# Early V loads into idle K buffers, and gathers in float32, in an attention and squared-ReLU kernel on one core

## The chip, the cores and the metric

The kernel runs on one core of a Trainium2 chip. The metric is device microseconds of one execution, median of three runs. TensorE is PE here, VectorE DVE, ScalarE ACT, GpSimd POOL; SyncE (SP) only issues DMAs.

## The reference

Batch 8, 8 heads, 576 positions, head size 64, 8 global positions. Attention within a window of 32 positions to either side, with 8 global rows and columns, then a dense layer to 2048, a squared ReLU and a dense layer back to 512:

```
scores = q @ k.T / sqrt(64)
mask   = (abs(i - j) <= 32) | is_global[i] | is_global[j]
attn   = softmax(where(mask, scores, -1e9)) @ v        # (8, 8, 576, 64) float32
x      = attn.transpose(0, 2, 1, 3).reshape(4608, 512)
out    = (s * relu(x @ w_in)**2 + b) @ w_out           # w_in 512x2048, w_out 2048x512
```

## The kernel before

The attention goes by pairs of heads: 32 pairs, counted from 0, four to a batch. A pair has five column chunks of 120 keys, with the 8 global keys in front of each (120 + 8 = 128 rows). Of a pair, `qk` (L530) makes the scores of a chunk on PE, ACT takes the exponent (`em` of pairs 0 to 4 at L544, `e` of later ones at L547; DVE multiplies those with a mask at L548), and `pvq` (L550) multiplies with V. `norm_steps` (L577) divides by the sums and puts the result into `xt`, the input of the dense layers. These run on PE as small pieces ("quanta", `moe_quanta` L644): L659 for x @ w_in into `psh`, ACT's L681 and DVE's L684 for the squared ReLU, L693 for the second product. A number of quanta stands behind each chunk of attention, so that PE has work while ACT and DVE are busy. All engines run in the order in which the code is written; every instruction waits for those it depends on by semaphores, and an engine that waits holds up all that stands behind it on that engine.

Inputs come in three ways.

- K and Q of pairs 0 to 7 are loaded as six rows to a partition into `six` (pair 0 on the hardware queues, 1 to 7 by `load_kq` L166 on POOL's queue, cast to bfloat16 on the way). K of pairs 8 and on is loaded in float32 into `natk` (four slots, `load_nat` L174, on SP's queue), cast by ACT into `natb` (`round_k` L199) and transposed by a DMA (`turn_k` L233). K of pair 8 is the first that goes this way; it is loaded at pair 4 and cast in chunk 1 of pair 6. So slots of `natk` are idle until then, but for pair 0's K at the start, which uses slot 0 and part of slot 1.
- V of every pair is loaded in float32 into `natv` (four slots, two DMAs of 150 KB to a pair) and cast into `vring` (five slots) by ACT or POOL: `cast_v` L242. V of pair 4 goes into slot 0, which is free when V of pair 0 has been cast. Rows 0 to 7 of `natv` are filled once (L267) with any numbers, since the cast reads all 128 rows; `put_v` (L435) then overwrites them in `vring` with the global rows.
- The rows of K, Q and V at the global positions are gathered by indirect DMAs on POOL's queue (`gather` L312) into `gf`, cast to bfloat16 on the way. `globals_of` (L397) gives the steps that turn them: PE transposes (L409), DVE copies (L413, L416).

POOL's queue also brings `w_in` (two halves, `load_w_in`) and `w_out` (four quarters, `load_w_out`). SP's and POOL's DMAs take turns on 8 semaphores each: a DMA waits until the one 8 before it on its queue has landed.

The first part of the program is `first_pair` (L848) for pairs 0 to 4. Within it ACT casts V of pair 0 (in chunk 1), POOL V of pairs 1 to 3 (L962 to L965), and ACT V of pair 4 in the last chunk of pair 4 (L879), followed by V of pair 5 (L793) and then by the first ReLUs. SP's queue holds V of pairs 0 to 6, then two fills with zeros (L998, L1001: rows 96 to 127 of the Q tiles and of `natb`; the first waits for PE's transposes of pair 5), V of pair 7, then K, Q and V of pairs 8, 9, 10 and so on. In chunk 1 of pair 6, ACT casts V of pair 6 and then K of pair 8.

Of the kernel before, what the change touches and what calls it, by code (L numbers as in the profile page):

```python
# [9 lines left out]
FP32 = mybir.dt.float32  # L10
# [6 lines left out]
P = 128  # L17
B, H, S, D = 8, 8, 576, 64
NG = 8
# [50 lines left out]
def kernel(  # L70
# [95 lines left out]
    def load_kq(p):  # L166
        bi, hp = divmod(p, 4)
        for t in "kq":
# [3 lines left out]
            )  # L172

    def load_nat(eng, t, p):  # L174
        bi, hp = divmod(p, 4)
        if t == "q":
            dst = natq[:].rearrange("p n h j d -> p n (h j d)")[:, :, 0 : NCH * 2 * D]
            dst = dst.rearrange("p n (c h d) -> p n c h d", c=NCH, h=2)
        else:
            dst = natv if t == "v" else natk  # L180
        r = NG if t == "v" else 0
        for hh in range(2):
            o = src[t][bi, 2 * hp + hh, 0, 0].offset

            runs = [(0, NCH, KC)]
            if p == NPAIR - 1 and hh == 1:
                runs = [(0, NCH - 1, KC), (NCH - 1, 1, S - KC * (NCH - 1))]
            for c, nch, n in runs:
                eng.dma_start(  # L189
                    out=dst[r : r + n, p % NV, c : c + nch, hh],  # L190
                    in_=bass.AP(
                        tensor=src[t].tensor, offset=o + c * KC * D,
                        ap=[[D, n], [KC * D, nch], [1, D]],
                    ),
                )
# [43 lines left out]
    def load_v(eng, p):  # L239
        load_nat(eng, "v", p)  # L240

    def cast_v(eng, p):  # L242
        eng(out=vring[:, p % NVR], in_=natv[:, p % NV])  # L243

# [28 lines left out]
    )  # L273
    load_v(nc.sync, 0)
    load_v(nc.sync, 1)
    load_v(nc.sync, 2)
    load_v(nc.sync, 3)

# [33 lines left out]
    def gather(bb, ts="kq"):  # L312

        if bb not in gfs:
            gfs[bb] = globp.tile([P, 3, D], BF16, tag="gf", name="gf")
        for t in ts:
            i = "kqv".index(t)
            nc.gpsimd.indirect_dma_start(
                out=gfs[bb][:, i], out_offset=None,
                in_=src[t].rearrange("b h s d -> (b h s) d"),  # L320
                in_offset=IndirectOffsetOnAxis(ap=grow[bb][:], axis=0),
            )
# [74 lines left out]
    def globals_of(bb):  # L397

        gb = gfs[bb]
        gkt[bb] = globp.tile([P, D], BF16, tag="gkt", name="gkt")  # L400
        if bb == 0:
            gvx[0] = const.tile([NG, 16 * D], BF16, name="gvx", tag="gvx")

        def turn():
# [27 lines left out]

        return turn, lambda: move(0), lambda: move(1)

# [492 lines left out]
    build_biases((0,))  # L927

    gather(0, "kqv")
    load_kq(3)  # L930
    load_kq(4)
# [18 lines left out]
    def clear6():  # L950
# [4 lines left out]
        0: [lambda: build_biases((1, 2)), clear6],  # L955
        1: [lambda: build_biases((3, 4)), lambda: cast_v(A, 0)],
        3: [clears],
        4: [lambda: select(1)],
    })
    flush()  # L960
    load_kq(5)
    cast_v(G, 1)  # L962
    cast_v(G, 2)
    load_w_in(1)
    cast_v(G, 3)  # L965
# [5 lines left out]
    load_w_out(1)  # L971
    load_v(nc.sync, 4)
    load_v(nc.sync, 5)
    load_v(nc.sync, 6)
    for p in (1, 2, 3, 4):
        first_pair(p, {
            2: [steps0[0]],
            4: [*steps0[1:], flush],
        } if p == 1 else {
# [14 lines left out]
    for i in (1, 2, 3):  # L994
# [8 lines left out]
        in_=view(dummy[96:P], [0, NV * NCH * P // DM], [1, DM]),  # L1003
    )
    load_v(nc.sync, 7)
    gather(1)
# [24 lines left out]
    for p in range(4, NPAIR):  # L1031
# [47 lines left out]
        if p % 8 > 4 and p + 3 < NPAIR:  # L1079
            if p % 8 == 6:  # L1080
                pass
            elif p % 8 == 7:
                at(3, globals_of((p + 3) // 8)[0])
        for s in {12: (2, 3, 4), 13: (7,), 14: (2, 4, 7)}.get(p, (2, 3, 4, 7)):
# [54 lines left out]
```

## Time and profile before

| what | number |
|---|---|
| time, median of 3 runs | 352.94 us (352.19 to 353.15) |
| the profiled execution: its own time, its span | 352.61 us, 350.9 us |
| busy share of the span: PE, DVE, ACT, POOL | 93%, 66%, 62%, 18% |
| shares of the chain that ended last | PE 81%, DVE 7%, DMA 5% |
| DMA: bytes, mean rate | 50.41 MB, 144 GB/s |
| share of 16 DMA engines, SP's queue and POOL's queue | 57.5%, 15.7% |

The shares are means over two very different stretches. Up to about 66 us the first pairs are set up, weights come in and PE has gaps; behind it PE is busy almost without a break. A DMA share over 1.00 in the windows means that packets of several queues were in flight on an engine at once. In the timelines "x2" are instructions merged into a row, and the brackets show how long the engine was idle before it and what ended that.

### The profile page before, as it was taken

Reading aid. Unit: us, or ns where it says so; the run is one execution under the profiler, and the core shown is the slowest. Engines: PE = TensorE matmul, PEld = TensorE weight load, DVE = VectorE, ACT = ScalarE, POOL = GpSimd, SP = SyncE. Lnnn points to the kernel's source line nnn. Section 1 sums busy time; section 2 is a strip of 40 time slices with the busy share of each in tenths; the row PEclk is TensorE's granted clock in tenths of the full one; section 3 lists DMA queues with packets and bytes.
Section 4 is the critical chain, followed back from the end, with each engine's and each line's share of the span. In section 5 each row is a group of like instructions: output and inputs, shape, how many; then the busy total and the mean of one; then the engine's idle time right before and its main releaser. Section 6 shows DMA issues by size and latency. Waiting matters only on the chain.

```text
span 350.9 us, 8468 instructions
## 1 busy us (share of the span) xinstructions
PE 327.3 (93%) x3130; PEld 172.7 (49%) x3175; DVE 231.8 (66%) x662; ACT 217.5 (62%) x453; POOL 64.4 (18%) x148
## 2 busy tenths in 40 slices
PE   5688698899999999999999999999999999999995
PEld 3244344355455444467645544554457544444444
DVE  6477766776868888877677767676767553413421
ACT  5458558746896579657875887588648604603600
POOL 7942641114001601130005000300020010000000
PEclk9999989999999999999999999999999999999999
DMA  8999999999997999999388877972530011011002
GB/s 168 210 204 198 189 199 202 200 174 223 178 186 157 216 198 192 210 168 175 50 184 203 206 159 152 262 178 67 157 111 2 2 62 61 1 61 60 0 34 89
DMA packets 125938, 50.41 MB, mean 144 GB/s; under 512 B 112544, under 2 KB 119360, under 8 KB 125888
## 3 DMA queue, kind: packets, MB, share of 16 engines
q1 hardware_dynamic: 116470, 38.78, 57.5%
q0 software_dynamic: 9072, 10.65, 15.7%
q8 instruction: 25, 0.41, 0.5%
q10 hardware_dynamic: 354, 0.43, 0.4%
q14 instruction: 17, 0.14, 0.1%
HBM read 42.27 MB, written 9.44 MB: 147 GB/s over the span
## 4 chain that ended last, share of the span: by engine, by line
PE 81%; DVE 7%; DMA 5%; issue 2%; ACT 2%; SPq 1%; another core or an unknown queue 1%; ACTq 0%; DVEq 0%
PE pso L693 32%; PE psh L659 32%; PE pss L535 6%; PE po L565 6%; DMA natk<-in_k_dram 4%; PE pst L461 1%; PE pst L474 1%; SPq L189 1%; DVE qbd L519 1%; DVE wsum L1016 1%; DVE kt L486 1%; DMA row<-in_moe_b_dram 1%; PE pss L534 1%; ACT em L544 1%
## 5 line engine op out<-in xcount | busy, mean ns | idle before, releaser
L659 PE MATMUL psh<-xt,win_t 128*128 128x512 bf16 (+4 forms) x685 | 136.7, 341 | 0.8 <-issue 0.2
L693 PE MATMUL pso<-wout_t,g 128*128 128x512 bf16 (+1 forms) x569 | 132.9, 373 | 2.1 <-issue 1.4
L681 ACT ACTIVATE r<-psh 128x512 bf16<-128x512 f32 x144 | 86.4, 602 | 59.2 <-PE psh L659 49.8
L659 PEld LDWEIGHTS <-win_t 128*128 128x128 bf16 x704 | 64.2, 98 | 57.8 <-issue 4.9
L684 DVE TENSOR_TENSOR g<-r 128x512 bf16<-128x512 bf16 x144 | 60.5, 431 | 39.6 <-ACT r L681 39.0
L693 PEld LDWEIGHTS <-g 128*128 128x128 bf16 x592 | 56.0, 98 | 59.1 <-issue 1.0
L547 ACT ACTIVATE e<-pss 128x384 bf16<-128x384 f32 (+2 forms) x135 | 62.8, 469 | 34.5 <-PE pss L535 31.7
L535 PE MATMUL pss<-qbd,kt 128*128 128x384 bf16 (+2 forms) x160 | 50.4, 318 | 9.9 <-DVE qbd L835 4.3
L548 DVE TENSOR_TENSOR em<-e,mask 128x384 bf16<-128x384 bf16 (+2 forms) x135 | 45.6, 339 | 14.7 <-ACT e L547 12.8
L636 POOL COPY xt<-xg 128x4 bf16 (+1 forms) x72 | 18.8, 262 | 174.9 <-DVE xt L611 169.2
L713 DVE SCALAR_TENSOR_TENSOR osb<-pso,spread,bias_row 128x512 f32<-128x512 f32 (+1 forms) x25 | 18.1, 726 | 29.7 <-PE pso L693 27.0
L535 PEld LDWEIGHTS <-kt 128*128 128x128 bf16 x160 | 15.7, 99 | 25.1 <-DVE qbd L835 4.0
L611 DVE TENSOR_TENSOR xt<-po,rep 128x480 bf16<-128x480 f32 (+2 forms) x60 | 24.3, 446 | 0.3 <-ACT rep L621 0.3
L514 DVE COPY qbd<-pst 64x600 bf16<-64x600 bf16 x38 | 17.8, 468 | 9.2 <-PE pst L461 8.6
L519 DVE COPY qbd<-pst 64x600 bf16<-64x600 bf16 x20 | 15.6, 780 | 5.8 <-PE pst L474 2.9
L200 ACT CAST natb<-natk 120x640 bf16<-120x640 f32 x24 | 17.7, 738 | 1.4 <-DMA natk<-in_k_dram 1.4
L544 ACT ACTIVATE em<-pss 128x384 bf16<-128x384 f32 (+2 forms) x25 | 11.1, 462 | 9.9 <-PE pss L540 5.2
L243 ACT CAST vring<-natv 128x640 bf16<-128x640 f32 x20 | 14.8, 742 | 3.8 <-DMA natv<-in_v_dram 3.8
L565 PE MATMUL po<-em,vring 128*32 128x160 bf16 (+3 forms) x840 | 16.9, 218 | 0.0
L618 ACT ACTIVATE ln<-po 128x324 f32<-128x324 f32 (+1 forms) x30 | 13.1, 435 | 3.8 <-PE po L565 3.8
L621 ACT ACTIVATE rep<-ln 128x324 f32<-128x324 f32 (+1 forms) x32 | 15.2, 475 | 0.1
L224 ACT CAST sixq<-natq 120x640 bf16<-120x640 f32 x19 | 14.3, 753 | 0.0
(124 smaller groups left out, 228.1 us busy)
## 6 DMA issues: line engine op xcount, KB each, us to landing
natv<-in_v_dram SPq DMA_DIRECT2D x63, 150.0 KB
natk<-in_k_dram SPq DMA_DIRECT2D x47, 150.0 KB
out_dram<-osb SPq DMA_DIRECT2D x23, 256.0 KB
natq<-in_q_dram SPq DMA_DIRECT2D x37, 150.0 KB
wst<-in_moe_w_out_dram POOLq DMA_DIRECT2D x8, 512.0 KB, 3.8
out_dram<-osbh SPq DMA_DIRECT2D x9, 256.0 KB
win_t<-in_moe_w_in_dram POOLq DMA_DIRECT2D x4, 512.0 KB, 12.4
wout_t<-in_moe_w_out_dram POOLq DMA_DIRECT2D x4, 512.0 KB, 10.5
```

The costliest lines, as they stand in the source:

```text
L519: eng(out=view(qbufs[p % 3][r, hh], [P, NCH], [HB + NG, 2], [NJ, n], [1, NJ]), in_=view(ps[r], [2 * n, NCH], [n, 2], [1, n], [NP6, NJ]),)
L535: nc.tensor.matmul(ps[:], ktile[p][:, P * c : P * c + P], qbufs[p % 3][:, :, LO[c] : HI[c]], start=p == 0 or p >= NCH, stop=p > 0,)
L547: nc.scalar.activation(e[:], ps[:], AF.Exp, scale=SCALE)
L548: later.append(lambda: nc.vector.tensor_mul(em[:], e[:], masks[c]))
L565: nc.tensor.matmul(po[DH * j : DH * j + DH, a : a + n], view(vring[:, p % NVR, c, hh, part - 1 :], [2, DH]) if part else onesb[:], emt[(p, ...
L611: nc.vector.tensor_tensor(out=view(xt[:, 2 * g, x0 + t0 :], [NXT, 2], [w, runs], [1, w]), in0=view(po[:, STEP[blk] + col :], [STEP[blk], 2 ...
L636: nc.gpsimd.tensor_copy(out=xt[:, h, S * (bi % NX) : S * (bi % NX) + S][:, :, ds(greg_p[i], 1)], in_=xgs[bi][:, h, i : i + 1],)
L659: nc.tensor.matmul(psh[:, d0 : d0 + n], win_t[:, a, f * P : f * P + P], xt[:, a, x0 : x0 + n], start=(a == 0 and j == 0), stop=(a == 3), s ...
L681: nc.scalar.activation(r[:], psh, AF.Relu)
L684: later.append(lambda g=g, r=r: nc.vector.tensor_mul(g[:], r[:], r[:]))
L693: nc.tensor.matmul(pso[:, 0:nn], gl[f][:, u * P : u * P + P], wout_t[:, f, n0 : n0 + nn], start=(f == 0), stop=(f == 15),)
L713: nc.vector.scalar_tensor_tensor(out=osb[:, 0:nn], in0=pso[:, 0:nn], scalar=s_bc, in1=bias_row[:, n0 : n0 + nn], op0=OP.mult, op1=OP.add,)
```

## The change

V of pairs 4 and 5 (the fifth and sixth) is loaded into slots 2 and 3 of `natk`, straight behind V of pair 3, so that it waits for no cast; a further small DMA fills rows 0 to 7 of these slots. V of pair 6 goes to `natv` behind the zero fills. The gathers keep float32, and a new DVE cast `round_g` makes the bfloat16 tile `gb`; the three gathers of batch 0 and 1 stand behind K and Q of pair 3 on POOL's queue. V of pair 0 is cast by POOL, not by ACT. The zero fills `clears` stand at chunk 2 of pair 0 in place of chunk 3, and the steps of `globals_of` are spread over chunks 1, 2 and 4 of pair 1.

```diff
+    def v_slot(p):
+        return p - 2 if p in (4, 5) else p % NV
...
             dst = natv if t == "v" else natk
-        r = NG if t == "v" else 0
+            if t == "v" and p in (4, 5):
+                dst = natk
+        r, n = (NG if t == "v" else 0), v_slot(p) if t == "v" else p % NV
...
     def cast_v(eng, p):
-        eng(out=vring[:, p % NVR], in_=natv[:, p % NV])
+        eng(out=vring[:, p % NVR], in_=(natk if p in (4, 5) else natv)[:, v_slot(p)])
...
-    load_v(nc.sync, 0)
-    load_v(nc.sync, 1)
-    load_v(nc.sync, 2)
-    load_v(nc.sync, 3)
+    nc.sync.dma_start(
+        out=natk[0:NG, 2:4].rearrange("p n c h d -> p (n c h d)"),
+        in_=bass.AP(
+            tensor=v.tensor, offset=v.offset,
+            ap=[[2 * NCH * 2 * D, NG], [1, 2 * NCH * 2 * D]],
+        ),
+    )
+    for p in range(6):
+        load_v(nc.sync, p)
...
-            gfs[bb] = globp.tile([P, 3, D], BF16, tag="gf", name="gf")
+            gfs[bb] = globp.tile([P, 3, D], FP32, tag="gf", name="gf")
...
-        gb = gfs[bb]
+        gb = globp.tile([P, 3, D], BF16, tag="gb", name="gb")
...
+        n = 2 if bb else 3
+
+        def round_g():
+            nc.vector.tensor_copy(out=gb[:, 0:n], in_=gfs[bb][:, 0:n])
...
-        return turn, lambda: move(0), lambda: move(1)
+        return round_g, turn, lambda: move(0), lambda: move(1)
...
+    load_kq(3)
     gather(0, "kqv")
-    load_kq(3)
     load_kq(4)
...
-        1: [lambda: build_biases((3, 4)), lambda: cast_v(A, 0)],
-        3: [clears],
+        1: [lambda: build_biases((3, 4))],
+        2: [clears],
...
+    cast_v(G, 0)
     cast_v(G, 1)
+    load_w_in(1)
     cast_v(G, 2)
-    load_w_in(1)
     cast_v(G, 3)
...
-    load_v(nc.sync, 4)
-    load_v(nc.sync, 5)
-    load_v(nc.sync, 6)
     for p in (1, 2, 3, 4):
         first_pair(p, {
-            2: [steps0[0]],
-            4: [*steps0[1:], flush],
+            1: [steps0[0]],
+            2: [steps0[1]],
+            4: [*steps0[2:], flush],
...
+    load_v(nc.sync, 6)
     load_v(nc.sync, 7)
...
             if p % 8 == 6:
-                pass
+                steps = globals_of((p + 4) // 8)
+                at(7, steps[0])
             elif p % 8 == 7:
-                at(3, globals_of((p + 3) // 8)[0])
+                at(3, steps[1])
```

SP's queue from the fill of `natv` to K and Q of pair 8, before (`natv<-in_v_dram` are V loads, two to a pair; `dummy` is the source of the zero fills):

```order
L267 DMA natv<-in_v_dram 8x2560
L189 DMA natv<-in_v_dram 120x5x64 x14
L998 DMA sixq<-dummy 32x10x384
L1001 DMA natb<-dummy 32x5x512
L189 DMA natv<-in_v_dram 120x5x64 x2
L189 DMA natk<-in_k_dram 120x5x64 x2
L210 DMA natq<-in_q_dram 96x2x384
```

The same stretch with the change:

```order
L272 DMA natv<-in_v_dram 8x2560
L279 DMA natk<-in_v_dram 8x1280
L194 DMA natv<-in_v_dram 120x5x64 x8
L194 DMA natk<-in_v_dram 120x5x64 x4
L1012 DMA sixq<-dummy 32x10x384
L1015 DMA natb<-dummy 32x5x512
L194 DMA natv<-in_v_dram 120x5x64 x4
L194 DMA natk<-in_k_dram 120x5x64 x2
L215 DMA natq<-in_q_dram 96x2x384
```

One small fill is added in front; of the 14 V loads in a row 12 stand there now, the last four of them into `natk`, and the two of pair 6 stand behind the zero fills, ahead of pair 7's.

POOL behind its loads for pair 2, before (`sixk`, `sixq` are K and Q of a pair, here of pairs 3 and 4; `gf` are the gathers):

```order
L318 DMA gf<-in_k_dram,grow_163 128x64
L318 DMA gf<-in_q_dram,grow_163 128x64
L318 DMA gf<-in_v_dram,grow_163 128x64
L169 DMA sixk<-in_k_dram 96x2x384
L169 DMA sixq<-in_q_dram 96x2x384
L169 DMA sixk<-in_k_dram 96x2x384
L169 DMA sixq<-in_q_dram 96x2x384
```

With the change:

```order
L169 DMA sixk<-in_k_dram 96x2x384
L169 DMA sixq<-in_q_dram 96x2x384
L328 DMA gf<-in_k_dram,grow_168 128x64
L328 DMA gf<-in_q_dram,grow_168 128x64
L328 DMA gf<-in_v_dram,grow_168 128x64
L169 DMA sixk<-in_k_dram 96x2x384
L169 DMA sixq<-in_q_dram 96x2x384
```

The three gathers went behind K and Q of pair 3. Further down, two V casts still stand ahead of the second half of w_in (of pairs 0 and 1 now, 1 and 2 before), and two behind it in place of one.

DVE in pair 1, from the copy of pair 2's Q to the next K, before (`gkt`, `gqd` are filled from PE's transposes `psg` of the gathered rows):

```order
L830 CAST kt<-psg 128x5x8
L835 CAST qbd_119<-psg 64x5x8 x2
L519 COPY qbd_120<-pst 64x5x2x60 x2
L413 COPY gkt<-psg 128x64
L416 COPY gqd_121<-psg 64x64 x2
L486 COPY kt<-pst 128x5x120
```

With the change:

```order
L845 CAST kt<-psg 128x5x8
L850 CAST qbd_119<-psg 64x5x8 x2
L534 COPY qbd_120<-pst 64x5x2x60 x2
L417 CAST gb<-gf 128x192
L428 COPY gkt<-psg 128x64
L431 COPY gqd_121<-psg 64x64 x2
L501 COPY kt<-pst 128x5x120
```

The new cast stands between the Q copies and the copy of `gkt`; PE's transposes, which stood ready by then, come behind it now. The zero fills of `clears` keep their place among DVE's instructions.

## Rows read from the trace of the kernel before

**Rows 1.** page, part 2: DMA busy (tenths) and GB/s, 40 slices
```profile
DMA  8999999999997999999388877972530011011002
GB/s 168 210 204 198 189 199 202 200 174 223 178 186 157 216 198 192 210 168 175 50 184 203 206 159 152 262 178 67 157 111 2 2 62 61 1 61 60 0 34 89
```

**Rows 2.** windows: start:end, length, busy us of each engine (instructions), PEclk, DMA, GB/s
```profile
36.00:40.80 4.80, 4.64 (x42) 2.14 (x41) 3.62 (x15) 1.01 (x2) 3.55 (x11) 1.00 1.16 207
40.80:44.20 3.40, 0.74 (x4) 0.39 (x4) 2.07 (x7) 3.32 (x8) 2.79 (x4) 1.00 1.18 161
44.20:47.60 3.40, 3.18 (x20) 1.42 (x18) 1.33 (x5) 2.06 (x6) 1.80 (x4) 0.50 1.24 199
51.00:55.00 4.00, 3.33 (x54) 1.68 (x53) 3.57 (x13) 3.23 (x7) 1.51 (x4) 1.00 1.16 220
57.10:62.60 5.50, 4.70 (x41) 2.02 (x40) 5.03 (x14) 4.47 (x10) 0.81 (x2) 1.00 1.04 213
66.00:350.90 284.90, 278.29 (x2488) 147.39 (x2524) 187.47 (x521) 176.44 (x364) 30.77 (x75) 1.00 0.65 132
```

**Rows 3.** timeline of ACT: start us, us, what, [idle before <-releaser]
```profile
15.46 0.72 ACT L243 CAST vring<-natv 128x640 bf16<-128x640 f32 x1
...
36.37 0.72 ACT L243 CAST vring<-natv 128x640 bf16<-128x640 f32 x1
40.88 0.72 ACT L243 CAST vring<-natv 128x640 bf16<-128x640 f32 x1 [3.79 <-DMA natv<-in_v_dram]
...
55.93 0.72 ACT L200 CAST natb<-natk 120x640 bf16<-120x640 f32 x1 [1.44 <-DMA natk<-in_k_dram]
```

**Rows 4.** timeline of PE, 40 to 65 us
```profile
40.20 0.59 PE L659 MATMUL psh<-xt,win_t 128*128 128x512 bf16 x2
43.45 0.32 PE L535 MATMUL pss<-qbd,kt 128*128 128x384 bf16 x1 [2.66 <-ACT e L547]
...
57.10 0.28 PE L535 MATMUL pss<-qbd,kt 128*128 128x272 bf16 x1 [0.75 <-ACT e L547]
...
62.62 0.47 PE L535 MATMUL pss<-qbd,kt 128*128 128x320 bf16 x2 [0.82 <-DVE qbd L449]
...
64.69 0.32 PE L535 MATMUL pss<-qbd,kt 128*128 128x384 bf16 x1 [0.73 <-ACT e L547]
```

**Rows 5.** chain of waits up to 70 us: start us, us, what
```profile
7.50 3.83 another core or an unknown queue
...
42.04 13.51 DMA natk<-in_k_dram
```

**Rows 6.** timeline of SP's queue: V of pair 4, K of pair 8
```profile
16.21 0.33 SPq L189 DMA_DIRECT2D natv<-in_v_dram  x1
...
42.04 4.69 SPq L189 DMA_DIRECT2D natk<-in_k_dram  x2
```

**Rows 7.** waits of SP's queue up to 70 us: us in total, times, longest
```profile
SPq L189 <- ACT vring L243: 4.0, 1, 4.0
SPq L998 <- PE pst L474: 3.4, 1, 3.4
```

**Rows 8.** timeline of DVE, 4 to 22 us
```profile
4.51 0.83 DVE L896 CAST sixk<-natk 96x768 bf16<-96x768 f32 x1
...
11.32 0.20 DVE L830 CAST kt<-psg 128x40 bf16<-128x40 f32 x1 [3.82 <-remote]
...
19.74 1.57 DVE L519 COPY qbd<-pst 64x600 bf16<-64x600 bf16 x2 [1.09 <-PE pst L474]
21.24 0.17 DVE L413 COPY gkt<-psg 128x64 bf16<-128x64 bf16 x1
```

**Rows 9.** timeline of PE, pair 1: transposes of the gathered rows
```profile
20.06 0.25 PE L409 MATMUL psg<-ident,gf 64*64 64x64 bf16 x4
```

**Rows 10.** timeline of POOL: first gather; casts of V
```profile
7.03 1.05 POOL L318 DMA_INDIRECT gf<-in_k_dram,grow  x1 [0.30 <-DVE kt L486]
...
16.10 1.40 POOL L243 CAST vring<-natv 128x640 bf16<-128x640 f32 x2
```

More of the change, by code (lines that the diff above doesn't have):

```diff
@@ L187, in load_nat @@
                 runs = [(0, NCH - 1, KC), (NCH - 1, 1, S - KC * (NCH - 1))]
-            for c, nch, n in runs:
+            for c, nch, rows in runs:
                 eng.dma_start(
-                    out=dst[r : r + n, p % NV, c : c + nch, hh],
+                    out=dst[r : r + rows, n, c : c + nch, hh],
                     in_=bass.AP(
                         tensor=src[t].tensor, offset=o + c * KC * D,
-                        ap=[[D, n], [KC * D, nch], [1, D]],
+                        ap=[[D, rows], [KC * D, nch], [1, D]],
                     ),
```

## The prediction

> **What bounds the kernel now.** I first read the windows of the whole trace. From 66 us on PE is busy for 278.29 of 284.90 us [rows 2], so nothing but the stretch ahead of 66 us can move the end by much: there PE has gaps, and whatever moves the moment at which PE gets its last late input moves the end by as much. Two more things are to be seen in that stretch. The DMA engines are busy nearly without a break: 9 tenths in slices 2 to 11 of the page, with 189 to 210 GB/s in each up to 70 us [rows 1], and a share of 1.16 or more in every window from 36 to 55 us [rows 2]. And the TensorE clock, which is 1.00 elsewhere, is 0.50 (1.2 in place of 2.4 GHz) from 44.2 to 47.6 us, just after a stretch of 3.4 us in which PE was busy for 0.74 us [rows 2].
>
> Then I looked for the gaps. PE stands still for 2.66 us from 40.79 to 43.45 us, waiting for ACT [rows 4]. ACT in turn had stood for 3.79 us in front of the cast of pair 5's V, whose DMA had not landed; it starts at 40.88 us [rows 3]. That is the wait at which the change aims. The next ones are 0.75 us at 57.10, 0.82 at 62.62 and 0.73 at 64.69 us [rows 4]. The first of them is a DMA's again: ACT waits 1.44 us for pair 8's K and casts it at 55.93 us [rows 3]. The chain of waits does not go through V of pair 5 at all. It goes through pair 8's K: 13.51 us from its issue at 42.04 us to its landing at 55.55 us [rows 5, 6]. So of two waits of ACT for a DMA the chain holds the second. This is the main thing in my forecast: the first wait is longer, but it ends 15 us earlier, and time won there only counts if pair 8's K comes earlier too.
>
> **The change part by part.** *V of pairs 4 and 5 earlier.* SP's queue stood 4.0 us for the cast of pair 0's V before it could issue pair 4's at 16.21 us [rows 6, 7]. With the slots in `natk` that wait is gone. If all behind it moves up by the 4.0 us, pair 5's V lands at 40.88 - 4.0 = 36.9 us; ACT is ready for it at 36.37 + 0.72 = 37.09 us [rows 3]. The wait is then gone. If the loads keep half of their gain (w_in's loads share the engines), it shrinks to 3.79 - 2.0 = 1.8 us. PE would get back up to 2.66 us of idle time and what the half clock took: PE was busy for 3.18 us of that window [rows 2], which at 2.4 GHz is 1.6 us of work, so 1.6 us. Together up to 4.3 us, between 37 and 55 us of the program.
>
> *Pair 8's K.* In SP's order V of pair 6 moves from ahead of the zero fills to behind them, but still stands ahead of K of pair 8. The same bytes go ahead of this K as before, and the engines were never idle before it. Added are the fill of `natk` (8 rows of 1280 float32, 41 kB) and the wider gathers (128 rows x 64 x 2 bytes more, three times, 49 kB): 90 kB, at 199 GB/s [rows 2] 0.45 us. Against that, the window from 40.8 to 44.2 us moved 161 GB/s where its neighbours moved 207 and 199 [rows 2]: about 40 GB/s x 3.4 us = 136 kB, 0.7 us, which a steadier flow can fill. So pair 8's K lands 0.25 us earlier by this, between 0.45 us later and 0.7 us earlier by its two terms. ACT and PE arrive there up to 4.3 us earlier, and wait. PE's 0.75 us there becomes about 4 us.
>
> *The clock.* A wait of 2.66 us was followed by half the clock [rows 2, 4]; one of 4 us will be too, now behind 55 us. In the window from 57.1 to 62.6 us PE is busy for 4.70 of 5.50 us, and DVE for 5.03 [rows 2]: DVE sets the pace there, and PE has 0.82 + 0.73 = 1.55 us of waiting up to 65 us that can absorb the 1.6 us of the slow stretch. Between 0 and 1.6 us, I take 0.2, by the waits that are there to be filled.
>
> *The gathers and the new cast.* The new cast of 128x192 stands between two measured ones, 0.20 us for 128x40 and 0.83 for 96x768 [rows 8]; by their columns some 0.33. PE's transposes at 20.06 us [rows 9] must now come behind it. DVE ends its Q copies at 21.31 us; then cast 0.33 and transposes 0.25, so `gkt` comes some 0.6 us later than its 21.24 us [rows 8]. PE waits too. Below: 0, if the stage reaches DVE earlier. It delays the zero fills of SP, which wait for PE [rows 7], by up to 0.6 us, while the DMA engines still work off w_out; hence I count it at 0, and at 0.6 if that cover is gone. In pairs 6, 14 and 22 the same cast stands in stretches where PE is never short: nothing. The gathers go behind two loads for pair 3 and land some 2 us later; they are needed by 21 us. Nothing.
>
> *V of pair 0 on POOL.* ACT loses 0.72 us at 15.46 us [rows 3], where it waits for PE afterwards anyway; POOL's casts cost 0.70 us each [rows 10], and POOL's next loads queue up behind others. `clears` keeps its place in DVE's order. Both nothing.
>
> Sum against the profiled execution's own 352.61 us: -0.25 + 0.2 = -0.05, so 352.56, 0.4 under the median of 352.94, whose runs spread over 0.96 us. I forecast 352.6, no change that can be measured; 0.3% is 1.06 us and about what a measurement of this kernel can tell.
>
> The Trainium skill has a rule that speaks against the change. TensorE: Matmul & The Clock Gate, in HAM oscillation, says that a wait for a DMA in front of dense matmuls makes them start at half the clock, and that the cost returns with every such wait. The trace agrees at 44.2 us (0.50). By that rule a long wait at pair 8's K would be paid in full; this is the second rival.
>
> **The rivals.** *The early wait counts in full.* If pair 8's K lands 4 us or more earlier (because the queue ahead of it is served better, or because the unexplained wait at 7.50 us goes), PE keeps what it wins: 2.66 + 1.6 + 0.75 - 0.6 = 4.4 us, 348.2 us. That wait of 3.83 us, in which DVE stood before `kt` at 11.32 us, began when POOL issued the first gather, at 7.03 us [rows 5, 8, 10]. For this rival speaks that SP gets 4.0 us earlier to everything behind; against it the full DMA engines [rows 1]. 14%. In between, with K of pair 8 1 to 3 us earlier: some 350.8 us, 20%.
>
> *Slower: a late K and a slow clock.* PE arrives early at pair 8's K and waits more than the 2.66 us that were enough for the half clock; the K itself lands 0.45 us later for the added bytes and 0.6 us for the later zero fills; and PE's slow stretch is not covered by DVE: 1.6 us. Sum 2.7 us, 355.3 us. It decides as soon as K lands no earlier and more than 1 us of the slow stretch shows. For it speaks that the clock did fall at 44.2 us [rows 2]; against it that DVE is the busier engine behind 57 us. 26%.
>
> *The change doesn't do what it says:* V of pair 5 still lands at 38 us or later, the wait shrinks to 1.8 us, and pair 8's K decides as before: 352.6 us, no change. It is within the likeliest case's result; 8% of the 40% below.
>
> **How the numbers follow.** Forecast (K of pair 8 decides, no change) 40%, its own range 351.4 to 354.0; full gain 14%; partial gain 20%; slower 26%. Of the forecast's 40 some 2 end below 351.88 and 2 above 354.0. Of the partial gain 3 stay within 0.3%. Of the slower case 2 stay within it. So faster 14 + 17 + 2 = 33, slower 24 + 2 = 26, same 41. The range from 349.2 to 355.2 us leaves out most of the full gain and the upper part of the slower case, some 2 in 10.
>
> **What would show it.** In the profile after: no wait of ACT before the two V casts at 37 us, and a clock of 1.00 from 44 to 48 us (the first step). ACT's wait before the first cast of `natk` into `natb` grows from 1.44 to about 5 us, ending near 55.5 us, with PE idle before it and a clock of 0.50 behind it (the second and third). The DVE cast of `gb` takes 0.2 to 0.8 us, and PE's transposes behind it start some 1.5 us later than 20.06 (the fourth). I am wrong if that cast of pair 8's K starts more than 1 us before 54.9 us, or if the chain of waits no longer holds the K loads.

## The result and the profile after

The changed kernel takes 354.87 us (median of 20 runs, 352.64 to 357.61) against 352.88 us before (20 runs, 352.16 to 354.81); the ratio is 1.0056, 95% interval 1.0035 to 1.0078. It is slower by some 2 us; I had forecast no change. The profiled execution took 356.62 us (span 354.9 us against 350.9), so its 4.0 us are more than the usual loss; a second profile (e11) is shown beside it below. Ratios leave out executions far above a kernel's fastest and medians do not, so for e17 and e19 the two differ.

The page of the changed kernel, DMA busy and GB/s in 40 slices, to be laid beside [rows 1]:
```profile
DMA  9999999999999899999099867983440011011002
GB/s 157 219 202 199 165 194 188 184 190 178 204 192 166 186 200 221 209 176 174 21 177 235 194 145 164 247 192 78 151 129 2 2 61 60 0 60 60 0 32 89
```
Slices are 8.9 us long: the fifth, from 35.5 to 44.4 us, has 165 GB/s where it had 189. The windows of [rows 2], in the same columns, place it:
```profile
36.00:40.80 4.80, 4.16 (x40) 2.00 (x41) 4.51 (x18) 2.66 (x7) 2.61 (x10) 1.00 1.02 174
40.80:44.20 3.40, 2.42 (x13) 1.13 (x13) 2.88 (x9) 3.38 (x8) 3.10 (x3) 1.00 0.99 148
44.20:47.60 3.40, 3.19 (x72) 1.87 (x73) 2.06 (x6) 2.07 (x6) 3.10 (x4) 1.00 1.13 160
...
57.10:62.60 5.50, 2.80 (x19) 0.98 (x20) 2.39 (x5) 3.97 (x9) 0.72 (x1) 0.50 0.89 184
66.00:350.90 284.90, 280.17 (x2495) 148.16 (x2532) 190.27 (x529) 178.62 (x368) 31.64 (x76) 1.00 0.66 133
```
In the first three the engines move 174, 148 and 160 GB/s where they moved 207, 161 and 199: (207 - 174) x 4.8 + 13 x 3.4 + 39 x 3.4 = 335 kB less, 1.7 us at 199 GB/s. The shortfall lies there alone: up to 36 us the two kernels move 195 (before) and 194 GB/s, from 36 to 48 us 191 and 163, and from 48 us to the landing of pair 8's K 201 and 204. The clock is 1.00 at 44 to 48 us now, and 0.50 at 57 to 63.

ACT's casts that wait for a DMA, answering to [rows 3]: V of pairs 4 and 5, V of pair 6, K of pair 8:
```profile
37.30 0.72 ACT L248 CAST vring<-natk 128x640 bf16<-128x640 f32 x1
40.06 0.72 ACT L248 CAST vring<-natk 128x640 bf16<-128x640 f32 x1 [2.04 <-DMA natk<-in_v_dram]
52.63 0.72 ACT L248 CAST vring<-natv 128x640 bf16<-128x640 f32 x1 [1.20 <-DMA natv<-in_v_dram]
58.63 0.72 ACT L205 CAST natb<-natk 120x640 bf16<-120x640 f32 x1 [5.27 <-DMA natk<-in_k_dram]
```
The wait for V of pair 5 fell from 3.79 to 2.04 us; the one for pair 8's K rose from 1.44 to 5.27 and ends 2.70 us later. PE's timeline, for [rows 4, 9], with waits of 0.98, 5.89 and 0.73 us where there were 2.66, 0.75 and 0.73; ahead of them the transposes of the globals, which waited for nothing listed before:
```profile
20.38 0.25 PE L424 MATMUL psg<-ident,gb 64*64 64x64 bf16 x4 [1.75 <-DVE gb L417]
...
42.63 0.32 PE L550 MATMUL pss<-qbd,kt 128*128 128x384 bf16 x1 [0.98 <-ACT e L562]
...
59.80 0.39 PE L550 MATMUL pss<-qbd,kt 128*128 128x272 bf16 x1 [5.89 <-ACT e L562]
67.89 0.32 PE L550 MATMUL pss<-qbd,kt 128*128 128x384 bf16 x1 [0.73 <-ACT e L562]
```
PE is 0.82 us early at 42.63 us, 2.70 late at 59.80, 3.20 late at 67.89 (the half clock took 0.5). The SP queue's timeline, for [rows 6, 7], says why:
```profile
13.82 8.84 SPq L194 DMA_DIRECT2D natk<-in_v_dram  x4
38.25 0.76 SPq L1012 DMA_DIRECT2D sixq<-dummy  x1
39.06 0.60 SPq L1015 DMA_DIRECT2D natb<-dummy  x1
39.76 5.09 SPq L194 DMA_DIRECT2D natv<-in_v_dram  x4
44.89 6.76 SPq L194 DMA_DIRECT2D natk<-in_k_dram  x2
```
SP is through with the issue of its last early V load at 22.66 us and then stands for 15.6 us before the zero fills, until PE has done with the transposes of pair 5. Before, V of pair 6 stood ahead of them, so this wait was 3.4 us [rows 7]. Now V of pairs 6 and 7 comes behind them instead of pair 7's alone, and pair 8's K is issued at 44.89 instead of 42.04 us. The chain of waits goes through these transposes, the fills, SP's issues and the DMA of pair 8's K, and through a second DMA far behind:
```profile
37.84 0.66 PE pst L489 x24
...
39.06 0.60 SPq L1015
...
42.52 2.33 SPq L194
44.89 2.95 SPq L194
47.88 10.68 DMA natk<-in_k_dram
...
145.76 6.37 DMA wst<-in_moe_w_out_dram
```
The last is a piece of w_out for `wsum`; DVE waits 0.72 us for it at 152 us, PE behind DVE 0.92 us, and that makes the 3.2 us of 68 us the 4.0 us of the end. The front, for [rows 8], DVE's timeline of the changed kernel:
```profile
8.05 0.20 DVE L845 CAST kt<-psg 128x40 bf16<-128x40 f32 x1 [0.36 <-PE psg L839]
...
17.92 1.57 DVE L534 COPY qbd<-pst 64x600 bf16<-64x600 bf16 x2 [1.82 <-PE pst L489]
19.41 0.91 DVE L417 CAST gb<-gf 128x192 bf16<-128x192 f32 x1
```
The wait of 3.82 us at the start is gone (8.05 instead of 11.32 us) and the Q copies come 1.82 us earlier. But the new cast takes 0.91 us, PE stands 1.75 us for it, and its clock is 0.50 from 22.15 to 25.56 us; the zero fills, at 37.32 us before, come at 38.25.

### The profile page after: what moved, and what is told of

Its sections match the earlier page's. It is cut to its first block, busy times and chain, and to the rows that moved or that the text cites. A ratio compares the mean times of both kernels' runs of the same rounds, so it can differ in the third digit from the quotient of the medians.

```text
span 354.9 us, 8471 instructions
## 1 busy us (share of the span) xinstructions
PE 330.4 (93%) x3130; PEld 173.8 (49%) x3175; DVE 234.2 (66%) x666; ACT 217.0 (61%) x452; POOL 67.6 (19%) x149
## 3 DMA queue, kind: packets, MB, share of 16 engines
q0 software_dynamic: 8064, 10.80, 15.6%
## 4 chain that ended last, share of the span: by engine, by line
PE 77%; DVE 7%; DMA 6%; issue 4%; SPq 3%; ACT 2%; POOL 0%; ACTq 0%; POOLq 0%; DVEq 0%
PE pso L708 30%; PE psh L674 29%; PE pss L550 6%; PE po L580 5%; DMA natk<-in_k_dram 3%; SPq L194 2%; DMA wst<-in_moe_w_out_dram 2%; DVE wsum L1031 1%; PE pst L476 1%; PE pst L489 1%; DVE g L699 1%; PE pss L549 1%; DMA row<-in_moe_b_dram 1%; DVE qbd L529 1%; DVE em L563 1%
## 5 line engine op out<-in xcount | busy, mean ns | idle before, releaser
L550 PE MATMUL pss<-qbd,kt 128*128 128x384 bf16 (+2 forms) x160 | 51.2, 323 | 9.5 <-ACT e L562 7.6
L534 DVE COPY qbd<-pst 64x600 bf16<-64x600 bf16 x20 | 15.6, 780 | 6.5 <-PE pst L489 3.6
L248 ACT CAST vring<-natv 128x640 bf16<-128x640 f32 x17 | 12.7, 745 | 1.2 <-DMA natv<-in_v_dram 1.2
## 6 DMA issues: line engine op xcount, KB each, us to landing
win_t<-in_moe_w_in_dram POOLq DMA_DIRECT2D x4, 512.0 KB, 11.1
```

The costliest lines, as they stand in the source:

```text
L550: nc.tensor.matmul(ps[:], ktile[p][:, P * c : P * c + P], qbufs[p % 3][:, :, LO[c] : HI[c]], start=p == 0 or p >= NCH, stop=p > 0,)
```

## Experiments

All ratios are to the kernel before, measured beside it. I began with three theories: SP's queue that runs empty (1), the slow front (2), the slow second batch of gathers on POOL (3). In the expectations from e5 on, theory A is 1 and 2 together (a late front and an empty queue), B the cast by itself, C the early V loads by themselves, and D, in e9, the place of the gathers.

**e1, V of pair 6 ahead again** (in the changed kernel):
```diff
     load_w_out(1)
+    load_v(nc.sync, 6)
 ...
-    load_v(nc.sync, 6)
     load_v(nc.sync, 7)
```


> The changed kernel with the one load of pair 6's V put back ahead of the two zero fills in SP's order (behind pair 5's V), all else as changed. Theory 1 (the empty queue): SP has nothing to issue for 15.6 us, then issues four loads ahead of pair 8's K; with V of pair 6 back in front, K of pair 8 is issued about 2 us earlier (some 43 us instead of 44.89) and lands near 56.3 us instead of 58.56, so PE's wait before pair 8's mask is about 3.5 us instead of 5.89, and the time falls by 2 to 2.5 us, to some 352.6. Theory 2 (the slow front: new cast on DVE and half a clock from 22 us, 0.93 us late from 26 us on): K of pair 8 comes at the same time as in the changed kernel, within 0.5 us, since the same bytes stand ahead of it; time 354 to 355. Theory 3 (the slow gather of 3.12 us on POOL at 42 us holds w_out and with it everything behind): no change either, 354 to 355, with the gather still near 3 us.


Measured: 354.54 us, 1.0042 (1.0014 to 1.0070). Pair 8's K landed at 56.2 us, as theory 1 said, but the time hardly fell: PE still waited 4.03 us there, and the clock was 0.50 from 56.71 to 63.53 us.
```profile
57.44 0.39 PE L550 MATMUL pss<-qbd,kt 128*128 128x272 bf16 x1 [4.03 <-ACT e L562]
```
POOL's gather took 2.65 us here, and in e2, e6 and e7 2.5 to 3.3 us with no loss of time: theory 3 falls.

**e2, V of pair 6 behind** (the reverse, on the kernel before, nothing else).


> The kernel before with only the load of pair 6's V moved behind the zero fills (V of pairs 4 and 5 stay in their old buffers, gathers in bfloat16). Theory 1: K of pair 8 is issued some 2 us later (44 instead of 42.04) and lands some 1.8 us later, near 57.4 us; the wait for pair 5's V stays near 3.8 us and ends where it ended, so the time rises by 1.5 to 2 us, to some 354.6. Theory 2: no difference, 352.9, since the front is that of the kernel before. Theory 3: no difference, as the gathers here are those of the kernel before.


Measured: 353.24 us, 1.0007 (0.9987 to 1.0028): nothing. Theory 1 alone falls. SP stood for 14.8 us before the zero fills here, about as long as in the changed kernel, but its front was early and they came at 33.85 us: it is not the length of that wait that counts, but when it ends.

**e3, gathers in bfloat16, no cast** (in the changed kernel; `round_g` goes, `gb` is `gfs[bb]`).


> The changed kernel with the gathers in bfloat16 again (still behind the fourth K and Q loads) and without the new cast on DVE in any batch; PE's transposes stand where they stood in the kernel before. Theory 1: the front to 26 us is 0.5 to 0.9 us ahead of the changed kernel, but K of pair 8 still stands behind V of pair 6 and 7; it lands at most 0.9 us earlier, 57.7 to 58.5 us, time 354.0 to 354.9. Theory 2: the 0.93 us and what follows from them go: zero fills near 37.2 us, K of pair 8 near 56 us, time 352.3 to 353. Theory 3: only if the gather of batch 2 on POOL falls from 3.12 to about 1 us does the time fall, by up to 1 us. Besides: if the wait of 3.83 us at the start (DVE before its first copy of k, at 7.5 us) hangs on the order of the gathers and not on their type, it stays away here too.


Measured: 353.52 us, 1.0018 (0.9994 to 1.0042). 1.3 us better than the changed kernel, zero fills at 34.48, K of pair 8 at 55.25 us.

**e4, K and Q of pair 8 ahead of the zero fills** (in the changed kernel):
```diff
     load_w_out(1)
+    load_nat(nc.sync, "k", 8)
+    load_q(8)
 ...
-                load_nat(nc.sync, "k", j)
-                load_q(j)
+                if j > 8:
+                    load_nat(nc.sync, "k", j)
+                    load_q(j)
```


> The changed kernel with the loads of pair 8's K and Q put ahead of the zero fills, directly behind pair 5's V in SP's order (their slots are free since the start); V of pair 6 stays behind the zero fills. Theory 1: SP's queue is not empty from 22.65 us on, pair 8's K has landed by 45 us, ACT's wait for it is 0, the next late ones are V of pair 6 (waited for 1.2 us) and K of pair 9; the time falls by 3 us or more against the changed kernel, to 350 to 352, below the kernel before. Theory 2: PE keeps the 0.93 us of the front as a loss, but the rest of the loss goes too: 352 to 353. Theory 3: w_out and the gathers come later still for the added bytes ahead, and the time stays at 354 or above.


Measured: 353.50 us, 1.0023 (0.9997 to 1.0049). K landed at 48.1 us and was not waited for. PE waited for the fill of the Q tiles in its place, and ACT cast V of pair 6 (second load landed at 54.0 us) without a wait of its own: the wait went to another DMA.
```profile
52.21 0.23 PE L489 MATMUL pst<-ident,sixq 100*64 100x100 bf16 x2 [3.24 <-DMA sixq<-dummy]
```

**e5, both repairs** (e1 and e3 together); **e6, only V of pairs 4 and 5** (that part alone, on the kernel before); **e7, only the cast** (float32 gathers and `round_g` on the kernel before).


> The changed kernel with both repairs: V of pair 6 ahead of the zero fills again, and the gathers in bfloat16 without the new cast. What stays of the change: V of pairs 4 and 5 in the idle K buffers, the gathers behind the fourth loads, the moved V cast and clears. Theory A (the DMA engines run dry, which takes both a late front and an empty SP queue): neither is left, pair 8's K lands near 55 us, when some 10.9 MB have been moved, and the time is that of the kernel before, 352.3 to 353.3. Theory B (the new cast costs by itself, through PE's wait of 1.4 us and the half clock behind it, the V load nothing): the same as with the bfloat16 gathers alone, 353.5. Theory C (the early V loads themselves cost, by a longer wait at pair 8's K and half the clock behind it): 353.8 or above.

> The kernel before with only V of pairs 4 and 5 loaded into the idle K buffers, ahead in SP's order (V of pair 6 stays ahead of the zero fills, the gathers where and what they were). Theory A: PE's wait for V of pair 5 shrinks, pair 8's K lands within 0.5 us of 55.5, PE's wait there grows by what the first lost; time 352.4 to 353.4, no change. Theory B: no change either, 352.9. Theory C: the longer wait at pair 8's K is followed by half the clock, and about 0.9 us of it shows: 353.8.

> The kernel before with only the gathers in float32 and the new cast of gb on DVE ahead of PE's transposes (in all three batches); the order of the loads stays that of the kernel before. Theory A: the front gets 0.9 us later (PE waits 1.4 us in place of 0.7 for the globals' keys), but V of pair 6 still stands ahead of the zero fills, the queue does not run dry, and pair 8's K lands within 0.5 us of 55.5: time 352.6 to 353.6. Theory B: 0.9 us for the cast, and up to 2 with half a clock behind it: 353.8 to 354.9.


Measured: e5 353.89 us, 1.0018 (0.9986 to 1.0051); e6 352.83 us, 0.9984 (0.9963 to 1.0005); e7 353.50 us, 0.9999 (0.9971 to 1.0027). None of the three parts run alone on the kernel before (e2, e6, e7) costs anything that can be measured; the moved V cast and `clears` were not run alone, and e5 holds them. e6 is the cleanest support of my main argument: V of pair 5 landed at 30.3 us, ACT did not wait for it, PE was 2.8 us earlier at 40.62 us, then stood 5.30 us for pair 8's K, which landed at 55.96 us (55.87 before), and nothing was left of it.
```profile
40.62 0.32 PE L545 MATMUL pss<-qbd,kt 128*128 128x384 bf16 x1 [0.38 <-ACT e L557]
...
57.19 0.38 PE L545 MATMUL pss<-qbd,kt 128*128 128x272 bf16 x1 [5.30 <-ACT e L557]
```

**e9, gathers first again** (`gather(0, "kqv")` ahead of `load_kq(3)` in the changed kernel); **e11 and e12, the changed kernel and the kernel before once more**.


> The changed kernel with one thing undone: the gathers stand ahead of the fourth K and Q loads in POOL's order again (float32, new cast, V of pair 6 behind the zero fills all stay). Theory D (the fourth K and Q loads, 6.70 us instead of 10.60, fill the engines' queues, so that SP issues V of pairs 4 and 5 only behind w_in's first loads: V of pair 5 landed at 40 us in every kernel with this order and at 30.3 us in the kernel with the V loads alone): V of pair 5 lands near 30 us again, no wait of ACT for it, and the time falls by about 1.2 us against the changed kernel, to 353.3 to 354. Theory A (empty queue and late front) and B (the cast): the time stays within 0.5 us of the changed kernel's, 354.4 to 355.4, since cast and queue are as they were; by theory A it may even rise, as SP's queue runs empty earlier.

> The changed kernel once more, as it is, beside the others on the same chip: a second profile. Theory A: the zero fills come near 38 us again, the DMA engines move under 180 GB/s between 36 and 48 us, and pair 8's K lands near 58 us. If what the first profile showed (the new cast of 0.91 us, half a clock from 22 to 25.6 us) was chance, the front is some 2 us earlier, the queue does not run dry, pair 8's K lands near 56 us, and the time of this execution is under 354. Median of all: 354.9 again.

> The kernel before once more, as it is: a second profile. If the stall of 3.83 us in which DVE stood at the start (7.50 to 11.32 us) belongs to the order of the gathers, it is there again. If it is chance (the kernel with only V of pair 6 moved had the same start without it), it is absent or of another length, the front up to 36 us is up to 3.5 us earlier, and the time is the same, 352 to 354, because pair 8's K lands near 55.5 us either way.


Measured: e9 354.58 us, 1.0048 (1.0018 to 1.0079): theory D falls, V of pair 5 came at 37.1 us, not at 30. ACT did not wait for it even so (it cast V of pairs 4 and 5 from 37.55 us on), and the time stayed. e11 354.72 us, 1.0040 (1.0013 to 1.0067), its profile 356.29: zero fills 38.67, 152 GB/s, pair 8's K at 58.03 us, so the first profile was no chance. e12 (353.54 us) had no stall at the start:
```profile
8.70 0.20 DVE L830 CAST kt<-psg 128x40 bf16<-128x40 f32 x1 [0.36 <-PE psg L824]
...
17.18 1.57 DVE L519 COPY qbd<-pst 64x600 bf16<-64x600 bf16 x2 [1.10 <-PE pst L474]
```
So the 3.82 us of [rows 8] come and go in one and the same kernel, and 2.6 us of an earlier front (17.18 against 19.74) bought nothing in the end: 1.5 us of it were left at 64 us, and DVE's waits for `wsum`'s pieces (2.34 us at 138.78) took more than that.

**e14, cast and V of pair 6 together** (e2 and e7 on the kernel before, nothing else).


> The kernel before with two parts of the change together, each of which alone cost nothing: the float32 gathers with the new cast, and V of pair 6 behind the zero fills (no V in the K buffers, the gathers' place as before). Theory A (late front and empty queue together): zero fills later than 36 us, under 190 GB/s between 36 and 48 us, pair 8's K near 57 to 58 us, time 354 to 355. In the kernel before, V of pair 5 lands later than in the changed one, so SP's queue is empty for less long, and the effect may be half as large: 353.8. Rival (something else in the change is needed: the early V loads, which empty SP's queue sooner): pair 8's K near 55.5 us and 353.0 to 353.5, as with either part alone.


Measured: 356.49 us, 1.0074 (1.0035 to 1.0113): two edits that cost nothing each cost 0.7% together. Its one profile has a wait of 3.18 us at the start, as the kernel before has and e2's and e7's have not, so only a part of its late front is the cast's. Zero fills are SP's first one; GB/s are those of the window 36 to 48 us; then when ACT starts to cast pair 8's K:

| kernel | cast | V6 behind | zero fills | GB/s | pair 8's K | ratio |
|---|---|---|---|---|---|---|
| before | no | no | 37.32 | 191 | 55.93 | 1 |
| e7 | yes | no | 36.50 | 188 | 55.73 | 0.9999 |
| e2 | no | yes | 33.85 | 203 | 55.12 | 1.0007 |
| e14 | yes | yes | 39.21 | 168 | 58.31 | 1.0074 |
| e1 | yes | no | 38.23 | 194 | 56.27 | 1.0042 |
| e3 | no | yes | 34.48 | 199 | 55.32 | 1.0018 |
| changed | yes | yes | 38.25 | 163 | 58.63 | 1.0056 |
| e9 | yes | yes | 38.50 | 156 | 58.35 | 1.0048 |

The window of e7, then that of e14:
```profile
36.00:48.00 12.00, 10.73 (x128) 5.42 (x128) 9.62 (x28) 7.93 (x18) 10.62 (x17) 1.00 1.23 188
```
```profile
36.00:48.00 12.00, 8.91 (x108) 4.52 (x110) 9.64 (x33) 8.49 (x19) 8.63 (x18) 1.00 1.04 168
```
The DMA share falls from 1.23 to 1.04 with both. From 38 to 42 us it is 0.78 to 0.93 in the four profiles with both and zero fills behind 38 us (e14, changed, e9, e11), and 1.08 to 1.23 in the others of the table and in e15. In e14 the engines are nearly idle for a moment: these are tenths in slices of 0.05 us, from 40 to 42 us.
```profile
DMA  5233130322122869597994979889779779699897
```
Either SP comes to its fills early (33.85 us in e2, 34.48 in e3), however long it stood, or V of pair 6 feeds the engines meanwhile; only without both do they run low.

**e15, PE kept busy in the gap; e17, the zero fills on POOL** (both in the changed kernel):
```diff
-            2: [steps0[1]],                     # e15
+            2: [lambda: warm(6), steps0[1]],
-    nc.sync.dma_start(                          # e17, both fills
+    nc.gpsimd.dma_start(
```


> The changed kernel with six matmuls of zeros (128x512 each, some 0.21 us at the full clock, into the spare bank) put ahead of PE's transposes of the globals, in the gap of 1.2 to 3 us in which PE waits for the new cast. If the half clock behind the gap is what makes the front late (theory A, its first half), the clock stays at 1.00 to 26 us, the front is 1.5 to 2 us ahead of the changed kernel's at 26 us, the zero fills come at 36 to 37 us, pair 8's K at 56 to 57 us, time 353.2 to 354. Rival (the wait itself and the DMA loads make it late, not the clock): the zero fills stay at 38 us and the time at 354.5 to 355.

> The changed kernel with the two zero fills issued by POOL (behind the third quarter of w_out) in place of SP; cast, V loads and all orders else as changed. Theory A, its second half: SP no longer waits for PE, issues V of pair 6, 7 and K of pair 8 some 8 us earlier, the engines do not run dry though the front is as late as in the changed kernel, pair 8's K lands before 55 us, time 352 to 353.5. Rival (the late front itself costs, through all that follows on PE): pair 8's K comes early, but the time stays at 354 to 355.


Measured: e15 355.29 us, 1.0056 (1.0026 to 1.0086). The clock stayed at 1.00 to 56.67 us, zero fills came at 37.19, the window moved 190 GB/s, pair 8's K was cast at 56.14 us: all as theory A said, and the time did not fall. PE waited 4.03 us, and by the starts of ACT's exponentials against those of before it lost another 0.95 us in the half clock behind that (56.67 to 63.50 us), 0.4 near 70 us, and 0.8 at 150 us, where DVE waits for `wsum`'s piece. e17 358.18 us, 1.0011 (0.9974 to 1.0048), inconclusive as a time. Its profile shows the second half of theory A: 203 GB/s, pair 8's K at 47.8 us. But the fill itself, behind w_out in POOL's queue, became the late one:
```profile
53.99 0.30 PE L489 MATMUL pst<-ident,sixq 100*64 100x100 bf16 x2 [5.03 <-DMA sixq<-dummy]
```

**e8, e10, e16, e18, e19, towards a faster kernel.** e8: both repairs, K and Q of pair 8 ahead, w_out's second quarter later. e10: e6 with two additions to `wsum` later. e16, against e6 (V of pairs 4 and 5 in the K buffers), has K and Q of pair 8 ahead, w_out's second quarter later, and the additions of e10:
```diff
-    load_w_out(1)
     load_v(nc.sync, 6)          # V of pairs 4, 5 already loaded into natk
+    load_nat(nc.sync, "k", 8)
+    load_q(8)
 ...
     load_kq(7)
+    load_w_out(1)
     load_w_out(2)
 ...
-        for s in {12: (2, 3, 4), 13: (7,), 14: (2, 4, 7)}.get(p, (2, 3, 4, 7)):
+        for s in {12: (2, 3, 4), 13: (7,), 14: (2, 4, 7), 15: (2, 3, 5, 7), 16: (2, 3, 7), 17: (2,)}.get(p, (2, 3, 4, 7)):
```
e18 is e16 with the cast, e19 is e16 with V of pairs 4 and 5 in their old buffers.


> The kernel with both repairs (V of pair 6 ahead of the zero fills, bfloat16 gathers), and besides the loads ordered by when they are used: K and Q of pair 8 also ahead of the zero fills, and the second quarter of w_out, used from some 63 us on, moved behind the seventh K and Q loads instead of ahead of the zero fills. Theory A (before 66 us the end is set by how early the last needed bytes come, in order): V of pair 5 lands near 36 us, pair 8's K near 42 us, PE has no wait over 1 us between 37 and 60 us, and the next late load is w_out near 63 us; the time falls to 349 to 351. Rival (the sum of the bytes up to 66 us decides, whatever their order): PE's waits move behind 60 us, to w_out or V of pair 9, and the time stays at 352 to 353.5.

> The kernel with V of pairs 4 and 5 alone in the K buffers (352.83 us against 353.23 of before), and besides two of the additions of w_out to wsum later: in pair 15 from the fifth mask to behind it, in pair 16 one to pair 17. If the wait of DVE for the last pieces of w_out (0.1 to 2 us of the span between 135 and 152 us, different in each profile) takes part in the scatter of the times, this wait is gone and the time falls by 0.3 to 0.8 us and scatters less: 352.0 to 352.6. Rival: that stretch's DMA engines are full, and another load (K for a transpose, V) is late there instead: 352.8.

> The kernel before with V of pairs 4 and 5 in the K buffers, K and Q of pair 8 behind V of pair 6 and ahead of the zero fills, the second quarter of w_out behind the seventh K and Q loads, and the two additions to wsum later; gathers and casts as before. If both waits that follow the DMA engines are moved (pair 8's K, and wsum's pieces behind 135 us), the gain of some 2 us at 66 us that the ordered loads showed is kept to the end: 350.0 to 351.5. Rival (a later load decides: w_out at 63 us, or another at 140 us): 352 or above, no better than 352.09.

> The kernel with the loads in order of use (349.68 us, ratio 0.988), and in it the float32 gathers and the new cast on DVE, nothing else. Theory A (a later front delays the zero fills, and these all that stands behind them, V of pair 7 and K of pair 9): PE waits 1.2 to 1.8 us for the globals in place of 0.72, the clock may fall to half for 3.4 us behind it, and of these 0.7 to 2 us stays to the end: 350.4 to 351.7. Rival (the cast is hidden, as its cost alone on the kernel before, 0.9999, says): 349.4 to 350.

> The kernel with the loads in order of use, but V of pairs 4 and 5 in their old buffers, waiting for the casts of pairs 0 and 1 as in the kernel before. If the early V loads are worth what the first step of the prediction says once pair 8's K no longer decides, PE waits 2 to 4 us for V of pair 5 near 41 us again (and for half a clock behind it), and the time is 352 to 353.5. If the w_out quarter that now comes behind them was what made V of pair 5 late, it lands near 36 us in the old buffers too, the wait is under 1 us, and the time is 349.5 to 350.5.


Measured: e8 352.87 us, 0.9964 (0.9929 to 0.9999); e10 352.09 us, 0.9976 (0.9952 to 0.9999); **e16 349.68 us, 0.9882 (0.9843 to 0.9921)**; e18 350.39 us, 0.9922 (0.9890 to 0.9954); e19 352.71 us, 0.9919 (0.9879 to 0.9960). e16 beats both kernels by more than 3 us. In its ACT timeline V of pairs 4 and 5 and pair 8's K are cast with no wait:
```profile
37.44 1.34 ACT L248 CAST vring<-natk 128x640 bf16<-128x640 f32 x2
50.87 0.74 ACT L248 CAST vring<-natv 128x640 bf16<-128x640 f32 x1
51.49 0.74 ACT L205 CAST natb<-natk 120x640 bf16<-120x640 f32 x1
```
PE has one wait over 0.4 us between 40 and 66 us (0.62), and the clock stays at 1.00. Some of the 4.9 us that it is ahead at 64 us goes again: 1.1 us up to 90 us, and 1.1 us at 142 us, where DVE waits 1.58 us for `wsum`'s piece; 2.8 us are left. e18 is 0.7 us above e16, with overlapping intervals: near the expected 0.7, not shown. In e19 the wait for V of pair 5 is back, and a new one:
```profile
42.32 0.32 PE L535 MATMUL pss<-qbd,kt 128*128 128x384 bf16 x1 [2.33 <-ACT e L547]
...
50.01 0.23 PE L474 MATMUL pst<-ident,sixq 100*64 100x100 bf16 x2 [2.97 <-DMA sixq<-dummy]
```
What the early V loads are worth there is not shown: the medians of e16 and e19 differ by 3 us, but the executions of e19 lie far apart (348.07 to 354.38), and by the ratios it is 1.3 us, with intervals that overlap.

## Why the prediction was wrong

*What bounds the kernel: right up to 66 us, not behind.* Pair 8's K decides the first stretch: e6 is 4.5 us ahead of the kernel before at 53 us, by the starts of ACT's exponentials, and 0.1 us behind it at 57. But that "nothing but the stretch ahead of 66 us can move the end by much" does not hold. Between 74 us and the end e3, e7 and e12 lose 2.4 to 3.1 us against before, where DVE waits 1.94, 2.37 and 2.34 us for a piece of w_out near 139 us. A lead at 66 us need not reach the end.

*V of pairs 4 and 5: right in kind, too large.* Pair 5's V landed at 39.96 us, not 36.9, and 2.04 us of the wait stayed. Among kernels with early V loads this landing moved between 30.3 us (e6) and 41.6 us (e17) and did not decide the time. What sets it is open; the gathers' place does not (e9), and it moves without a change of the program: e10 differs from e6 only from pair 15 on and had it at 37.8 us.

*Pair 8's K: the step that failed.* I wrote that "the same bytes go ahead of this K as before, and the engines were never idle before it", and took 0.25 us earlier, at worst 0.45 later. Its cast came 2.70 us later. (The 55.55 us of the prediction is the landing of its first half; the second landed at 55.87 before and at 58.56 us here.) The loads are the same; the time at which they may start is not. V of pair 6 moved from one side of an instruction that waits for PE to the other, and was what the engines worked on during that wait. I read the 3.4 us of [rows 7] as the wait of an instruction and did not ask what the engines would work on if the wait ended later. By the windows 10.9 MB had been moved when this K landed before and 11.1 MB here: the 0.2 MB are 1.0 us at 204 GB/s (I had counted 0.09), and the shortfall between 36 and 48 us is the other 1.7. That the two parts together make this K late, and that they cost time together, is shown by e14 against e2 and e7.

*The cast: its own size right, what it costs the front too small, its cover wrong.* 0.33 us was near: 0.24 to 0.37 us in eight profiles of kernels with it, 0.91 and 1.83 in the changed kernel's and e9's. The 0.6 us for the front was near only where the clock stayed at 1.00. From pair 1's first exponential to pair 3's, ACT takes 9.80 us before (19.03 to 28.83) and 13.12 us in the changed kernel (16.65 to 29.77). The cast's kernels lose 0.7 to 0.8 us there in the three profiles in which the clock stays at 1.00 (e4, e14, e15) and 1.7 to 4.6 us in the seven in which it falls to half; of the ten without the cast nine lose nothing and e6 0.56. So a front that was 2.4 us ahead at 19 us was 0.9 us late at 29, and with it the zero fills. I counted what follows at 0 while "the DMA engines still work off w_out", and 0.6 if that cover is gone. The cover was V of pair 6's load, and the same change took it away.

*What stays open.* In e1 and e15 pair 8's K is nearly in time, and the kernel is still 1.5 to 2 us slower than before. So the late K is not the only way to the loss, and how much of the changed kernel's 2 us is the late K's is not shown: mending it alone wins nothing that can be measured (354.54 and 355.29 against 354.87 us). The profiles point to the half clock behind PE's wait. At 74 us the four with the late K (changed, e9, e11, e14) are 2.4 to 3.2 us behind the kernel before, e1 and e15 1.2 and 1.5, e6 0.1. In e1 and e15 the half clock reaches 6.1 and 6.2 us beyond the end of PE's wait of 4.03 us, and 0.9 us of it shows; in e6 it reaches 4.3 us beyond a wait of 5.30, and none of it shows; in the changed kernel it reaches 3.3 us beyond, and 0.5 shows. No run isolates this.

*The clock: the rule applied, and twice.* In the changed kernel it is 0.50 from 56.28 to 63.11 us, and 0.5 us showed (I took 0.2 of 0 to 1.6); in e1 and e15 0.9. I had not seen the other place: behind the gap of 1.2 to 3.0 us before the globals' transposes the clock went to half, between 19 and 23 us, in seven of nine profiles with the cast and this gap, and in none of the ten without it, where the gap is 0.73 us or less. The Trainium skill, TensorE: Matmul & The Clock Gate, HAM oscillation, has a wait for a DMA make the next stage start slowly, each time anew. Here the wait is for a cast, and seven of nine profiles agree. e15 adds that filling the gap kept the clock at 1.00 there.

*Moved V cast, clears, gathers behind loads: nothing,* as said, as far as the runs tell: e9 for the gathers, and e5, which has all three and the early V loads, with 1.0018 (0.9986 to 1.0051).

*The rivals.* "A late K and a slow clock", 26%, is what happened: 2.7 us forecast, 3.2 in the profile at 68 us and 2.0 in the medians. Its cause for the late K (added bytes 0.45, later fills 0.6) was too small, and that the K was late for engines that ran low was not in it; that it came near the number is in part luck. "The early wait counts in full", 348.2 us if pair 8's K lands 4 us earlier, is near e16's 349.68, where that K was moved ahead and other loads with it.

## What to carry to other kernels

An edit counted at nothing because something covers it must be checked against the other edits of the same change: here one took the cover of the other. In a queue that issues in order, a load moved behind an instruction that waits for an engine does not keep its place among the bytes; ask when that wait ends, and what the DMA engines have to do until then. And where several loads are late in turn, moving one shows only the next: order all of them by when they are used, then measure. A time won in an early stage is won only if no late load takes it back.

## What the runs showed of the hardware

The start has a wait of 2.6 to 3.8 us that comes and goes with no change of the program (3.82 in the profile of the kernel before, none in that of e12, the same kernel; e14 3.18, e16 3.17, e17 2.62 us). The new cast took 0.91 us in the changed kernel (19.41 to 20.32 us) beside two casts of V on POOL (18.78 to 20.22 us). The Trainium skill, SBUF — State Buffer, Who interferes with whom, says that a DVE instruction in a mode that uses both of its port pairs, as casts can, shares one pair with POOL, and that whichever comes first holds it for the whole instruction. These times would allow it. Others speak against it as the whole cause: e1's cast took 0.30 us at 19.91 us, beside POOL's casts of 18.68 to 20.11 us, and e9's 1.83 us began 0.98 us before POOL's cast at 18.77 us. And the same late loads hold DVE for different times: pieces of w_out near 140 to 152 us held it for at most 0.25 us at once before, 2.34 in e12 (the same kernel), 0.72 in the changed kernel and 1.94 in e3 (whose code from pair 8 on is that of before).
